# An attention and gated-MLP kernel: residual rows loaded during the attention products, input weights loaded in a chain, the last z2 normalised ahead of the weight scaling and stored from GpSimd's queue

## The chip, the cores and the metric

One core of a Trainium2 chip runs the whole kernel. The metric is the device time of one execution in microseconds (us); lower is better. A core has a matrix engine (PE, with its weight loads shown as PEld), a vector engine (DVE), a scalar engine (ACT), GpSimd (POOL), and a sync engine (SP) that mostly issues transfers. DMAs can be issued from SP, ACT and POOL; each of these queues works through its instructions in order, so an instruction that waits holds up all that stands behind it.

## The reference

Two blocks in a row on 2048 rows of 1024 columns, in bf16:

```
h   = x + attention(layernorm(x)) @ wo        # 32 heads of 32; each row sees 8 rows: itself, 2, 4 .. 14 back
z   = gelu(layernorm(h) @ w_in)               # 1024 -> 3584
z1  = z[:, :1792];  z2 = layernorm(z[:, 1792:])
g   = w_sp @ z2 + b_sp                        # w_sp is 2048 x 2048: it mixes the rows
out = h + (z1 * g) @ w_out                    # 1792 -> 1024
```

## The kernel before

The 2048 rows are worked in four chunks of 512 rows, and a chunk in four blocks of 128 rows. Up to line 1031 nearly all work is entered into a planner; after that comes the row-mixing product and the output projection, written out in order.

**The planner.** `Order` (line 69) takes operations with an engine, a cost in us, dependences with latencies, a priority (lower goes first) and slots (three PSUM accumulators `acc`, buffers and so on). `run` (line 85) plays the schedule with these costs and then calls the functions in order of planned start. So the order of instructions on every engine's queue follows from the planned times, not from when data really arrive. `dma_op` (line 396) is an operation of the pseudo-engine "DMA": its cost says how long a transfer is taken to last, and its function issues it at its planned start; with an empty function it is only a delay.

**Attention of a chunk** (`attention`, line 484). DVE forms q*k for eight shifts (L522 with the additions L526, L529, L532), PE sums over the head's columns (L552), softmax follows; the attention weights are spread to all partitions, the second half of them through HBM (`spread`, line 598). Then come eight products with v. The products with shifts 1 and 3 are added by DMAs issued from POOL (`gather`, line 651, into `av_y` and `av_oT`), the products 4 to 7 by DVE (`dm` L638, `plus` L646). The end is `G["avdone", c]`.

**Head of a chunk** (`head`, line 687). PE multiplies with `wo` (L709), four blocks, each in four parts. DVE adds the residual rows `xr` and sums (L718, `res`); the sum `hb` is stored to HBM (L720), ACT squares it (L723), and the normalised rows are transposed by DMA into `hnT` (L760; for the last chunk block by block, L741). `xr` has three buffers. Three blocks are loaded by `xr_load` (L713) when the first part of block 0's matmuls is emitted, the fourth after ACT has squared block 0.

**The weights of the first MLP product.** `load_win` (line 385) issues four loads from POOL's queue: k = 0 and 1 are the columns of z2, k = 2 and 3 those of z1; 2.0, 1.5, 2.0 and 1.5 MB. Loads 0 and 1 go into the buffers of q's and k's weights, so they can start when the last chunk's q and k products are done (lines 978, 979). Load 0 also waits for the spread of chunk 1 (`behind_spread`). Loads 2 and 3 are issued together by `open_` (line 971) when the last v product is done. Behind these loads on POOL's queue stands the load of v for chunk 2 (L493).

**z2 and z1** (`b_z2`, line 767; `b_z1`, line 842). For each block PE fills one accumulator with 1024 columns and one with 768 (L786); ACT applies gelu into `u` (L793) and squares it for the variance (L801); POOL takes the power -0.5 (L682). For chunks 0 to 2 the normalised z2 is written by ACT and stored from SP. For the last chunk (`each`) it is done block by block: DVE normalises (L820), and the store is issued from ACT's queue (L821). z1 follows with L852 and gelu L858.

**The row mixing's weights.** The rows of `w_sp` are transposed by DMA from SP into `rawa` and `rawb` (`load_raw`, L927), `rawa` in three pieces. DVE multiplies them with row factors (`scale_raw`, L932), forms four differences (`t_forms`, L939 to L945) and four forms of z2 (`z_form`, L962, from `z2f` loaded back at L954), and a bias row (L922); these are the inputs of a two-by-two block product with seven multiplications (L1051). In the last chunk the orders of these DVE operations come from the planner, with priorities 3.5 to 3.7 against 0.6 for L820.

Lines 1014 to 1017 give the raw loads' planned costs (2.2, 2.2, 5.5 and 9.0 us) and what they follow: a dependence `(G["hnT", 3, k], 0.0 - 3.9)` means "3.9 us before the planned end of block k's transpose", which lasts 4.0 in the plan, so just after its start.

Of the kernel before, what the change touches and what calls it, by code (L numbers as in the profile page):

```python
# [132 lines left out]
def kernel(  # L133
# [251 lines left out]
    def load_win(k, t):  # L385
        c0, wd = win_specs[k]
        i_ = dma_w(t[:], win_view[:, :, c0:c0 + wd])
        if k == 0:
            behind_spread(i_, 1)
        wins[k] = t  # L390

    o_ = Order({"PE": 22.4, "ACT": 23.6, "DVE": 15.4, "POOL": 12.0}, {"acc": 3, "L": 1, "prod": 1, "part": 2, "xn": 4})
# [88 lines left out]
    def behind_spread(i_, c):  # L481
        tc.add_manual_dep(i_.ins, G["spread_i", c].ins.name, wait_for, reason="keep a large load out of the spread weights' way")

    def attention(c):
# [174 lines left out]
        o_2 = dm(2, "oT", [z] + ([G["headmm", c - 1]] if c else []))  # L659
        z = dm(3, "zz", [o_2] + ([G["hnT", c - 1]] if c else []))  # L660
        g2 = gather("oT", "zz", [z], 15.0)
        prev = dm(4, "b", [z], take="prod")
        for w in (5, 6, 7):
            m_ = dm(w, "p", [prev], take="prod" if w == 5 else None, free="part" if w == 7 else None)
            prev = plus("b", "p", [m_], free="prod" if w == 7 else None)
# [21 lines left out]
    def head(c):  # L687
        last = c == NCH - 1
        st = {}
        hbs = []  # L690
        prio = 4.0 + c * 0.1
        xr0 = dma_op(0.0, lambda: None, [G["attq", c]] if ("attq", c) in G else [])
        sqd = []
        for il in range(TPC):
            i = c * TPC + il
            deps = [G["avdone", c]]
            for part in range(4):
                def mm(part=part, il=il, i=i):
                    if part == 0:
                        if il == 0:  # L700
                            st["hsum"] = bp.tile([P, TPC], FP32, name="hsum", tag="hsum")
                            st["hsq"] = bp.tile([P, TPC], FP32, name="hsq", tag="hsq")
                            st["hnc"] = bp.tile([P, TPC, D], BF16, name="hb", tag="hb", bufs=1)
                            for k in range(min(XRB, TPC)):
                                xr_load(k)
                        st["acc", il] = new_acc()
                    for dl in range(2 * part, 2 * part + 2):
                        for nh in range(2):
                            T.matmul(st["acc", il][:, nh, :], oTs[c][:, dl, il * P:(il + 1) * P], wo_sb[:, dl, nh * CH:(nh + 1) * CH],  # L709
                                     start=(dl == 0), stop=(dl == DLO - 1))  # L710
                def xr_load(k):
                    st["xr", k] = bp.tile([P, D], BF16, name="xr", tag="xr", bufs=XRB)
                    dma(st["xr", k][:], x2d[(c * TPC + k) * P:(c * TPC + k + 1) * P, :])  # L713
                m_ = add("PE", 0.8634, mm, deps, prio=prio + il * 1e-2 + part * 1e-3, take="acc" if part == 0 else None)
                deps = [(m_, 0.0)]
            def res(il=il, i=i):
                hb = st["hnc"][:, il, :]
                V.scalar_tensor_tensor(hb, st["acc", il][:].rearrange("p a b -> p (a b)"), 1.0, st["xr", il][:],  # L718
                                       op0=ALU.mult, op1=ALU.add, accum_out=st["hsum"][:, il:il + 1])
                dma(h_d[i * P:(i + 1) * P, :], hb)  # L720
            r_ = add("DVE", 1.15, res, [m_] + ([G["hdone", c - 1]] if c else []), prio=1.0, free="acc", lat=0.15)
            def hsq(il=il):
                A.activation(st["xr", il][:], st["hnc"][:, il, :], ACTF.Square, accum_out=st["hsq"][:, il:il + 1])  # L723
                if il + XRB < TPC:
                    xr_load(il + XRB)
            sqd.append(add("ACT", 1.12, hsq, [r_], prio=3.0, lat=0.25))
        G["headmm", c] = m_
        if last:
            G["close"] = dma_op(0.0, close_, [G["headmm", c]] + [G["z2n", k, il] for k in range(c) for il in range(TPC)])
            for il in range(TPC):  # L730
                rs = batch_rstd(("l2", c, il), lambda il=il: st["hsum"][:, il:il + 1], lambda il=il: st["hsq"][:, il:il + 1],
                                D, f"l2_{il}", [sqd[il]], 0.5, cols=1)
                def nrm(il=il):
                    t = G["l2", c, il]
                    V.tensor_scalar(st["hnc"][:, il, :], st["hnc"][:, il, :], t["nmean"][:], t["rstd"][:],
                                    op0=ALU.add, op1=ALU.mult)
                n_ = add("DVE", 0.5, nrm, [rs], prio=0.6)
                def tr(il=il):
                    if il == 0:
                        hnTs[c] = bp.tile([P, TPC, KT, P], BF16, name="hnT", tag="hn%d" % (c % 2), bufs=1)  # L740
                    nc.sync.dma_start_transpose(hnTs[c][:, il], st["hnc"][:, il, :].rearrange("s (a p) -> s a p", p=P))  # L741
                G["hnT", c, il] = dma_op(4.0, tr, [n_])
            G["hnT", c] = G["hnT", c, TPC - 1]
            G["hdone", c] = n_
            return
        rs = batch_rstd(("l2", c), lambda: st["hsum"][:], lambda: st["hsq"][:], D, "l2", sqd, 0.5)
        nd = []
        for il in range(TPC):
            def nrm(il=il):
                t = G["l2", c]  # L750
                if il < L2DVE[c]:
                    V.tensor_scalar(st["hnc"][:, il, :], st["hnc"][:, il, :], t["nmean"][:, il:il + 1], t["rstd"][:, il:il + 1],
                                    op0=ALU.add, op1=ALU.mult)
                else:
                    A.activation(st["hnc"][:, il, :], st["hnc"][:, il, :], ACTF.Identity, scale=t["rstd"][:, il:il + 1], bias=t["nb"][:, il:il + 1])
            nd.append(add("DVE", 0.5, nrm, [rs], prio=0.6) if il < L2DVE[c] else add("ACT", 1.16, nrm, [rs], prio=4.0))
        G["hdone", c] = nd[-1]
        def tr():
            hnTs[c] = bp.tile([P, TPC, KT, P], BF16, name="hnT", tag="hn%d" % (c % 2), bufs=1)
            nc.sync.dma_start_transpose(hnTs[c][:].rearrange("p il a s -> p (il a) s"),  # L760
                                        st["hnc"][:].rearrange("s il (a p) -> s (il a) p", p=P))
        G["hnT", c] = dma_op(8.0, tr, nd)
# [4 lines left out]
    def b_z2(c):  # L767
# [43 lines left out]
        for il in range(TPC):  # L811
# [5 lines left out]
            def nrm(il=il, i=i, part=1):  # L817
                if each:
                    t = G["l3", c, il]
                    V.tensor_scalar(st["u", il][:], st["u", il][:], t["nmean"][:], t["rstd"][:], op0=ALU.add, op1=ALU.mult)  # L820
                    A.dma_start(z2_d[i * P:(i + 1) * P, :], st["u", il][:])  # L821
                    return
                t = G["l3", c]
                z2 = st["u", il]
                if Z2ACT[c] > il:
                    cols = slice(part * FH // 2, (part + 1) * FH // 2)
                    A.activation(z2[:, cols], st["u", il][:, cols], ACTF.Identity, scale=t["rstd"][:, il:il + 1], bias=t["nb"][:, il:il + 1])
                else:
                    V.tensor_scalar(z2[:], st["u", il][:], t["nmean"][:, il:il + 1], t["rstd"][:, il:il + 1], op0=ALU.add, op1=ALU.mult)
                if part:  # L830
                    dma(z2_d[i * P:(i + 1) * P, :], z2[:])
# [153 lines left out]
    for c in range(NCH):  # L985
        attention(c)
        if c == 1:
            G["win", 0].deps.append((G["spread", 1], 0.1))
        if c < NCH - 1:
            head(c)  # L990
    for c in range(NCH - 1):
# [19 lines left out]
    rl_ = dma_op(4.0, rows_first, [(ro_, 2.5), G["close"]])  # L1011
    b_z2(NCH - 1)
    b_z1(NCH - 1)
    r0_ = dma_op(2.2, lambda: load_raw(0, 0, 1), [G["close"], rl_.deps[0], (G["hnT", NCH - 1, 1], 0.0 - 3.9)])
    r0_ = dma_op(2.2, lambda: load_raw(0, 1, 2), [r0_, (G["hnT", NCH - 1, 2], 0.0 - 3.9)])
    r0_ = dma_op(5.5, lambda: load_raw(0, 2, TPC), [r0_, (G["hnT", NCH - 1, 3], 0.0 - 3.9)])
    r1_ = dma_op(9.0, lambda: load_raw(1), [r0_])
    prev = []
    for c, r_ in ((0, r0_), (1, r1_)):
        for k0 in (0, HK):  # L1020
            prev = [add("DVE", 2.3, lambda c=c, k0=k0: scale_raw(c, k0), [r_, rl_] + prev, prio=3.5)]
    for n in (0, 3, 1, 2):
        prev = [add("DVE", 2.3, lambda n=n: t_forms(0, n), prev, prio=3.6)]
    z_ld = {}
    for n in range(2):
        for hf in range(2):
            z_ld[n, hf] = dma_op(6.0, lambda n=n, hf=hf: load_z2f(n, hf), [r1_] + [G["z2st", 2 * hf + c, il] for c in range(2) for il in range(TPC)])
    for m in (3, 1, 2, 4):
        prev = [add("DVE", 0.7, lambda m=m: z_form(0, m), [z_ld[0, 0]] + ([z_ld[0, 1]] if m != 3 else []) + prev, prio=3.65)]
    add("DVE", 0.7, lambda: bias_rows(0), prev, prio=3.7)  # L1030
    o_.run()
    wout_a = wtile([P, 8, D], "wout_a", "wA")
# [188 lines left out]
```

## Time and profile before

| | us |
|---|---|
| runs shown: 714.1, 712.27, 713.95; median | 713.95 |
| the profiled execution | 714.85 |
| its span, first to last instruction | 712.9 |
| PE busy | 696.4 |
| DVE busy | 507.1 |
| ACT busy | 276.0 |
| POOL busy | 119.4 |
| mean granted clock of PE | 0.993 |

A line of the timeline gives start, duration, engine, line, operation, out<-in, shapes and a count of instructions merged; in brackets how long the engine stood idle before it and what released it. "SPq", "ACTq" and "POOLq" are the instructions of the queues themselves, such as the issue of a DMA. The stages of the profiled span, by what PE works on:

| us from the span's start | PE's work |
|---|---|
| 0 to 191 | q, k, v of all four chunks; chunk 0's `wo` product at 116 to 130 |
| 191 to 202 | z2 of chunk 0, first block |
| 202 to 216 | `wo` product of chunk 1 |
| 216 to 387 | z2 and z1 of chunks 0 to 2, `wo` products of chunks 2 (286 to 300) and 3 (372 to 386) |
| 387 to 418 | z2 of chunk 3, the last |
| 418 to 443 | z1 of chunk 3 |
| 443 to 710 | row mixing and output projection, twice |

Idle time of an engine that is not the one that others wait for costs nothing; here PE is busy for 98% of the span.

### The profile page before, as it was taken

The page shows a single profiled execution, that of the slowest core. Times are in us where ns is not written, and L with a number is a line of the kernel's source. Part 1 is how long each engine was busy: PE and PEld are TensorE (multiplying, and loading weights), DVE is VectorE, ACT ScalarE, POOL GpSimd, SP SyncE. Part 2 cuts the span into 40 slices and gives each one's busy share as a digit, 9 for nine tenths or more (in the row PEclk, how much of TensorE's full clock was granted, in tenths as well). Part 3 has the DMA queues.
Part 4 walks back from the last instruction along what each step waited for, and adds up shares of the span by engine and source line. Part 5 has one row for each costly group of instructions (what it writes and reads, how often), then busy time and mean ns, then how long its engine had stood idle before and what let it go on. Part 6 is the DMA issues. An engine that isn't in the chain of part 4 may idle for free.

```text
span 712.9 us, 8790 instructions
## 1 busy us (share of the span) xinstructions
PE 696.4 (98%) x3400; PEld 360.5 (51%) x3427; DVE 507.1 (71%) x614; ACT 276.0 (39%) x388; POOL 119.4 (17%) x109
## 2 busy tenths in 40 slices
PE   8999999999989999999999989999999999999998
PEld 7766665666535445444444434444444444444444
DVE  6899899999959899997985275555454965554322
ACT  4546652443317786755663262135410001111000
POOL 0100010012101111100301020343340023434000
PEclk9999999999999999999999989999999999999999
DMA  9978597577991569361675975568999416352121
GB/s 324 322 237 231 171 224 237 148 206 193 309 395 49 147 203 274 137 191 38 134 244 143 213 228 160 177 188 227 308 296 212 157 59 175 92 152 85 44 89 45
DMA packets 145545, 133.04 MB, mean 187 GB/s; under 512 B 68768, under 2 KB 117312, under 8 KB 145376
## 3 DMA queue, kind: packets, MB, share of 16 engines
q1 hardware_dynamic: 132784, 88.93, 44.5%
q0 software_dynamic: 7488, 31.13, 15.7%
q10 hardware_dynamic: 5232, 12.42, 5.1%
q8 instruction: 27, 0.44, 0.3%
q14 instruction: 14, 0.11, 0.0%
HBM read 75.24 MB, written 33.10 MB: 152 GB/s over the span
## 4 chain that ended last, share of the span: by engine, by line
PE 88%; DVE 6%; DMA 4%; issue 1%; ACT 1%; SPq 1%; ACTq 0%; DVEq 0%
PE bank L1051 24%; PE acc L459 21%; PE bank L1152 14%; PE acc L852 12%; PE acc L786 8%; PE acc L709 6%; DMA xr<-in_A_x_dram 2%; PE acc L303 2%; DVE prod L522 2%; DMA rawa<-in_B_w_sp_dram 1%; DVE prod L526 1%; DVE hb L718 1%; DVE prod L529 1%; DVE part L532 0%; DMA xp<-in_A_x_dram 0%
## 5 line engine op out<-in xcount | busy, mean ns | idle before, releaser
L786 PE MATMUL acc<-win,hnT 128*128 128x512 bf16 (+1 forms) x501 | 101.5, 361 | 9.3 <-ACT u L793 4.7
L852 PE MATMUL acc<-hnT,win 128*128 128x512 bf16 x448 | 98.0, 379 | 0.0
L786 PEld LDWEIGHTS <-hnT 128*128 128x128 bf16 x512 | 51.0, 100 | 58.9 <-issue 8.4
L522 DVE TENSOR_TENSOR prod<-qT,kT 128x4096 bf16<-128x4096 bf16 x32 | 72.7, 2283 | 1.3 <-ACT kT L465 1.3
L1152 PEld LDWEIGHTS <-zg 128*128 128x128 bf16 x462 | 44.6, 98 | 52.2
L1051 PEld LDWEIGHTS <-zs 128*128 128x128 f16 x448 | 43.8, 98 | 52.9
L852 PEld LDWEIGHTS <-win 128*128 128x128 bf16 x448 | 43.6, 98 | 52.5 <-issue 0.6
L470 ACT CAST stg<-acc 128x1024 bf16<-128x1024 f32 x36 | 36.4, 1012 | 61.2 <-PE acc L459 55.9
L1087 ACT COPY p<-bank 128x512 f32<-128x512 f32 x14 | 8.2, 586 | 132.0 <-PE bank L1051 129.6
L1152 PE MATMUL bank<-wout_a,zg 128*128 128x512 bf16 (+2 forms) x258 | 57.9, 373 | 0.3
L459 PE MATMUL acc<-xnT,wk 128*128 128x512 bf16 x256 | 56.5, 380 | 0.0
L709 PE MATMUL acc<-wo_sb,av_oT 128*128 128x512 bf16 x250 | 56.2, 381 | 0.3
L459 PE MATMUL acc<-xnT,wv 128*128 128x512 bf16 x256 | 56.1, 379 | 0.0
L1155 DVE SCALAR_TENSOR_TENSOR hr<-bank,rinv_w,hr 128x512 bf16<-128x512 f32 (+2 forms) x33 | 22.8, 730 | 44.8 <-PE bank L1152 43.6
L1051 PE MATMUL bank<-rawa,z2f 128*128 128x512 f16 x224 | 52.9, 379 | 1.1 <-ACT z1s L858 1.1
L1051 PEld LDWEIGHTS <-z2f 128*128 128x128 bf16 x336 | 32.8, 98 | 40.9 <-issue 1.4
L1051 PE MATMUL bank<-rawb,zs 128*128 128x512 f16 x224 | 52.9, 379 | 0.0
L1051 PE MATMUL bank<-form,zs 128*128 128x512 f16 x224 | 50.6, 379 | 0.0
L459 PEld LDWEIGHTS <-wv 128*128 128x128 bf16 x256 | 36.6, 143 | 18.6 <-issue 0.2
L459 PEld LDWEIGHTS <-wk 128*128 128x128 bf16 x256 | 36.5, 144 | 18.8 <-issue 0.7
L1152 PE MATMUL bank<-wout_b,zg 128*128 128x512 bf16 (+2 forms) x194 | 44.2, 373 | 0.2
L858 ACT ACTIVATE z1s<-acc 128x1024 bf16<-128x1024 f32 x28 | 28.6, 1022 | 38.0 <-PE acc L852 29.4
(188 smaller groups left out, 942.5 us busy)
## 6 DMA issues: line engine op xcount, KB each, us to landing
z2f<-z_d SPq DMA_DIRECT2D x28, 512.0 KB, 5.4
qkv_d<-stg SPq DMA_DIRECT2D x36, 256.0 KB, 3.8
wn<-in_B_w_sp_dram ACTq DMA_DIRECT2D x16, 512.0 KB, 3.7
z1c<-z_d SPq DMA_DIRECT2D x14, 512.0 KB, 4.1
z_d<-z1s SPq DMA_DIRECT2D x21, 256.0 KB, 2.2
z_d<-u SPq DMA_DIRECT2D x12, 448.0 KB, 2.5
av_y<-av_z POOLq DMA_DIRECT2D x4, 1024.0 KB, 9.8
av_oT<-av_zz POOLq DMA_DIRECT2D x4, 1024.0 KB, 15.1
```

The lines of the kernel that those rows point to most:

```text
L303: T.matmul(dst.rearrange("p (a b) -> p a b", b=P), wqs[:, kt, dl, :], xnT[0][:, lo:hi, kt, :], start=start, stop=stop)
L459: T.matmul(G[key][:, j, :].rearrange("p (a b) -> p a b", a=TPC), wv[:, kt, dl, :], xnT[c][:, :, kt, :], start=(kt == 0), stop=(kt == KT - 1))
L470: A.copy(stg[:], G[key][:])
L522: V.tensor_tensor(st["prod"][:], qT[:], kT[:, :, o:o + CH], op=ALU.mult)
L709: T.matmul(st["acc", il][:, nh, :], oTs[c][:, dl, il * P:(il + 1) * P], wo_sb[:, dl, nh * CH:(nh + 1) * CH], start=(dl == 0), stop=(dl == ...
L786: T.matmul(accf[:, n0:n1], hnTs[c][:, il, kt, :], wins[hf][:, kt, n0:n1], start=(kt == 0), stop=(kt == KT - 1))
L852: T.matmul(G["accy", c, fp][:, j, :].rearrange("p (a b) -> p a b", a=TPC), wt[:, kt, f0 * P:(f0 + 1) * P], hnTs[c][:, :, kt, :], start=(kt ...
L858: A.activation(z1s[:], G["accy", c, fp][:], ACTF.Gelu_apprx_tanh)
L1051: T.matmul(dst[:], wts[:, k, :], mov[:, k, :], start=(first and k == 0), stop=(k == HK - 1), skip_group_check=not first)
L1087: A.copy(p1[:], k1[:])
L1152: T.matmul(outs, zg[:, f, il * P:(il + 1) * P], wt[:, f0, lo:hi], start=(f == 0), stop=(f == NF - 1))
L1155: V.scalar_tensor_tensor(hr[:, lo:hi], acc[:, 0:hi - lo], rv[:, t:t + 1], hr[:, lo:hi], op0=ALU.mult, op1=ALU.add)
```

## The change

Four edits:

1. The first three residual blocks `xr` of each chunk are loaded by an operation of their own, planned right after DVE's product with shift 4 (`G["avmid", c]`), instead of with the first matmuls of `wo`.
2. The loads of the input weights 1 and 2 each wait for the one before (a dependence on its landing, in the program and in the plan). Load 3 follows load 2 without such a wait.
3. The store of z2 in the last chunk is issued from POOL's queue (`dma_w`) instead of ACT's.
4. The planned costs of the raw loads become 4.0, 4.0, 8.0 and 10.5 us; the first follows the transpose of block 2 instead of block 1, the second that of block 3 instead of block 2. The loads of z2 (`z_ld`) are entered earlier, and one z2 form is placed between the differences.

```
 def load_win(k, t):                                   # edit 2
         behind_spread(i_, 1)
+    elif k < 3:
+        tc.add_manual_dep(i_.ins, G["win_i", k - 1].ins.name, wait_for, reason="one load of input weights after the other")
+    G["win_i", k] = i_
...
+        G["win", 1].deps.append((G["win", 0], 0.1))
+        G["open"].deps.append((G["win", 1], 0.1))
...
-    prev = dm(4, "b", [z], take="prod")               # edit 1
+    prev = G["avmid", c] = dm(4, "b", [z], take="prod")
...
-    xr0 = dma_op(0.0, lambda: None, [G["attq", c]] if ("attq", c) in G else [])
+    def xr_load(k):
+        st["xr", k] = bp.tile([P, D], BF16, name="xr", tag="xr", bufs=XRB)
+        dma(st["xr", k][:], x2d[(c * TPC + k) * P:(c * TPC + k + 1) * P, :])
+    def xr_first():
+        for k in range(XRB):
+            xr_load(k)
+    xr0 = dma_op(4.0, xr_first, [G["avmid", c]] + ([G["hdone", c - 1]] if c else []))
...
-                A.dma_start(z2_d[i * P:(i + 1) * P, :], st["u", il][:])      # edit 3
+                dma_w(z2_d[i * P:(i + 1) * P, :], st["u", il][:])
...
-r0_ = dma_op(2.2, lambda: load_raw(0, 0, 1), [G["close"], rl_.deps[0], (G["hnT", NCH - 1, 1], 0.0 - 3.9)])   # edit 4
-r0_ = dma_op(2.2, lambda: load_raw(0, 1, 2), [r0_, (G["hnT", NCH - 1, 2], 0.0 - 3.9)])
-r0_ = dma_op(5.5, lambda: load_raw(0, 2, TPC), [r0_, (G["hnT", NCH - 1, 3], 0.0 - 3.9)])
-r1_ = dma_op(9.0, lambda: load_raw(1), [r0_])
+r0_ = dma_op(4.0, lambda: load_raw(0, 0, 1), [G["close"], rl_.deps[0], (G["hnT", NCH - 1, 2], 0.0 - 3.9)])
+r0_ = dma_op(4.0, lambda: load_raw(0, 1, 2), [r0_, (G["hnT", NCH - 1, 3], 0.0 - 3.9)])
+r0_ = dma_op(8.0, lambda: load_raw(0, 2, TPC), [r0_, (G["hnT", NCH - 1, 3], 0.0 - 3.9)])
+r1_ = dma_op(10.5, lambda: load_raw(1), [r0_])
...
-for n in (0, 3, 1, 2):
+for n in (0, 3):
     prev = [add("DVE", 2.3, lambda n=n: t_forms(0, n), prev, prio=3.6)]
+prev = [add("DVE", 0.7, lambda: z_form(0, 3), [z_ld[0, 0]] + prev, prio=3.6)]
+for n in (1, 2):
+    prev = [add("DVE", 2.3, lambda n=n: t_forms(0, n), prev, prio=3.6)]
-for m in (3, 1, 2, 4):
+for m in (1, 2, 4):
     prev = [add("DVE", 0.7, lambda m=m: z_form(0, m), [z_ld[0, 0], z_ld[0, 1]] + prev, prio=3.65)]
```

In head, L718 (`res`) now also depends on `xr0` in the plan.

More of the change, by code (lines that the diff above doesn't have):

```diff
@@ L703, in mm @@
                             st["hnc"] = bp.tile([P, TPC, D], BF16, name="hb", tag="hb", bufs=1)
-                            for k in range(min(XRB, TPC)):
-                                xr_load(k)
                         st["acc", il] = new_acc()
@@ L710, in mm @@
                                      start=(dl == 0), stop=(dl == DLO - 1))
-                def xr_load(k):
-                    st["xr", k] = bp.tile([P, D], BF16, name="xr", tag="xr", bufs=XRB)
-                    dma(st["xr", k][:], x2d[(c * TPC + k) * P:(c * TPC + k + 1) * P, :])
                 m_ = add("PE", 0.8634, mm, deps, prio=prio + il * 1e-2 + part * 1e-3, take="acc" if part == 0 else None)
@@ L720, in res @@
                 dma(h_d[i * P:(i + 1) * P, :], hb)
-            r_ = add("DVE", 1.15, res, [m_] + ([G["hdone", c - 1]] if c else []), prio=1.0, free="acc", lat=0.15)
+            r_ = add("DVE", 1.15, res, [m_, xr0] + ([G["hdone", c - 1]] if c else []), prio=1.0, free="acc", lat=0.15)
             def hsq(il=il):
@@ L1021 @@
             prev = [add("DVE", 2.3, lambda c=c, k0=k0: scale_raw(c, k0), [r_, rl_] + prev, prio=3.5)]
-    for n in (0, 3, 1, 2):
-        prev = [add("DVE", 2.3, lambda n=n: t_forms(0, n), prev, prio=3.6)]
     z_ld = {}
@@ L1027 @@
             z_ld[n, hf] = dma_op(6.0, lambda n=n, hf=hf: load_z2f(n, hf), [r1_] + [G["z2st", 2 * hf + c, il] for c in range(2) for il in range(TPC)])
-    for m in (3, 1, 2, 4):
-        prev = [add("DVE", 0.7, lambda m=m: z_form(0, m), [z_ld[0, 0]] + ([z_ld[0, 1]] if m != 3 else []) + prev, prio=3.65)]
+    for n in (0, 3):
+        prev = [add("DVE", 2.3, lambda n=n: t_forms(0, n), prev, prio=3.6)]
+    prev = [add("DVE", 0.7, lambda: z_form(0, 3), [z_ld[0, 0]] + prev, prio=3.6)]
+    for n in (1, 2):
+        prev = [add("DVE", 2.3, lambda n=n: t_forms(0, n), prev, prio=3.6)]
+    for m in (1, 2, 4):
+        prev = [add("DVE", 0.7, lambda m=m: z_form(0, m), [z_ld[0, 0], z_ld[0, 1]] + prev, prio=3.65)]
     add("DVE", 0.7, lambda: bias_rows(0), prev, prio=3.7)
```

## The prediction

> **What bounds the kernel now.** I read the page first. TensorE (PE) is busy for 696.4 of 712.9 us, so a change can only win back PE's idle time and time at a lowered clock. The list of PE's waits (us in total, times, longest) names the idle time that there is; it stands below the page's line:
>
> ```profile
> PE 696.4 (98%) x3400; PEld 360.5 (51%) x3427; DVE 507.1 (71%) x614; ACT 276.0 (39%) x388; POOL 119.4 (17%) x109
> ```
>
> ```profile
> PE acc L786 <- ACT u L793: 4.7, 1, 4.7
> PE acc L786 <- DMA win<-in_B_w_in_dram: 4.0, 1, 4.0
> ...
> PE bank L1051 <- ACT z1s L858: 1.1, 1, 1.1
> ...
> PE L L552 <- DVE part L532: 0.3, 1, 0.3
> ```
>
> Two waits count. I call the 4.0 us the first stall (after 194 us) and the 4.7 us the last-chunk stall (after 408 us). The table by stages shows the clock beside each (columns: PE, PEld, DVE, ACT, POOL busy, granted clock, DMA share, GB/s):
>
> ```profile
> 200.00:202.00 2.00, 2.00 (x8) 0.98 (x7) 0.82 (x1) 0.00 (x0) 0.00 (x0) 0.50 1.02 408
> ...
> 410.00:420.00 10.00, 6.87 (x26) 3.27 (x26) 6.92 (x14) 8.15 (x13) 0.88 (x2) 0.66 1.15 309
> ```
>
> After each stall the matmuls run at a granted clock of 0.5 to 0.7 for a few us, so a stall costs more than its wait. The rest of the last-chunk stall is in the timeline:
>
> ```profile
> 406.92 2.29 DVE L932 TENSOR_TENSOR rawa<-rawa,rows 128x4096 f16<-128x4096 bf16 x1 [10.91 <-DMA rawa<-in_B_w_sp_dram]
> 409.13 0.74 DVE L820 TENSOR_SCALAR u<-u,l_0nmean,l_0rstd 128x1792 bf16<-128x1792 bf16 x1
> ...
> 409.91 0.34 ACTq L821 DMA_DIRECT2D z_d<-u  x1
> 410.29 1.70 ACT L801 ACTIVATE junk<-u 128x1792 bf16<-128x1792 bf16 x1 [10.43 <-DVE u L820]
> ...
> 413.13 5.02 PE L786 MATMUL acc<-win,hnT 128*128 128x512 bf16 x16 [4.70 <-ACT u L793]
> ```
>
> Read it upwards. PE wants a free accumulator, which ACT's gelu (L793) frees. ACT stands at its own DMA instruction, the store of z2 (L821), which waits for DVE's normalisation L820. L820 has had its factor since 396.63 (POOL's L682 at 396.09 took 0.54), but it is queued behind L932, which waits for `rawa` until 406.92.
>
> **The last chunk's z2, step by step.** Both edits hit this. The store goes to GpSimd's queue, so ACT no longer stands behind it. And with the planner's new times for the raw loads (4, 4, 8, 10.5 us for 2.2, 2.2, 5.5, 9.0, each gated one transpose later or after the one before), the plan's `rawa` is due 0.1 + 4.0 + 8.0 and more, over 12 us after the last transpose's start instead of 0.1 + 5.5, while block 0's factor came 6.1 us after that transpose had its input (390.55 in the trace); so I expect L820 of block 0 to stand ahead of L932. The stall goes even if only the store moves. PE would run from 386.81: block 0 took 6.07 us (32 matmuls to 392.88), four take 24.3, end 411.1. In the trace z2 ends at 418.15. Its loss is 4.70 of waiting and 5.02 - 2.62 = 2.40 us at the low clock: **-7.1 us**. ACT keeps up: per block it needs 1.02 + 0.81 + 1.70 and three reads of 0.19, 4.1 us, below 6.07.
>
> What is late next? First the transposes `hnT` of blocks 2 and 3, on SP. The first raw load (4.03 us of SP) moves behind block 2's transpose, so that is issued near 389.2 instead of 393.49, and block 3's near 394.6 instead of 397.00. At 6.7 us to landing (the upper row of `hnT`) they are there at 396 and 401; PE wants them at 399 and 405. All raw loads together still end on SP near 412, so `rawb` lands near 416.4 as now. Then DVE's chain: from 416.4 the four remaining big operations (two scalings, of which one waits for block 3's norm, and so on) are 2 x 2.29 (L932), 0.74 (L820), 4 x 2.29 (L939 to L945), 4 x 0.69 (L962) and 0.68 (L922): 17.9 us, ending 434.3. PE reaches L1051 at 443.44 - 7.1 = 436.3, and wants the last forms 3 to 5 us later still. Now the same chain ends at 440.1 against 443.44, so the cover shrinks from 3.3 us to 2.0 and does not break.
>
> The store on GpSimd's queue: this trace has no such store. An issue there takes 0.88 to 1.27 us (L387, L493, L652) where ACT's took 0.34. Behind it on that queue stands only the next block's small L682. Landing: 2.5 us (the same rows on SP) or 4.3 (on ACT) on one end, 21.0 (`win` on GpSimd's queue, in a full stage) on the other; I take 4.3, the same store in the same stage, because the DMA share is 0.26 at 420 to 430. The last one is issued at about 420.4 and lands at 424.7; `z2f` follows in 5.4 (430.1); its first reader (L962, second form) is needed by PE at 439.7, so 0.7 + 5.4 back the store may land as late as 433.6: 13.2 us of landing are hidden. Cost 0.
>
> The row against this edit is L682: 0.54 us on an idle DVE, 2.52 at 419.66 and 426.14, beside a 2.28 us DVE operation. The Trainium skill, page "SBUF — State Buffer", section "SBUF: two separate sides", goes further: it warns that a DMA issued from GpSimd can't get its descriptors written while DVE runs in certain modes, and advises the ACT or SP queue. By that rule each of the four issues could be held to the end of a DVE operation, 2.3 us by the row; the last would land at 427 and still be hidden. The `win` issue at 172.16 took 0.95 us beside DVE's L635, which doesn't show it.
>
> **The chained weight loads.** I split the DMA view into 2 us windows and added up each queue's bytes. GpSimd's queue q0 works its transfers off one by one: the landings (issue plus time to landing) are `win` 0 at 188.0, the gather into `av_oT` 194.0, `win` 1 198.8, `win` 2 205.0, `win` 3 210.7, `vT` 214.2, in the order of issue, and the bytes between fit one transfer each. So `win` 1 (issued 177.79, landing 21.0 us later) is not slowed by `win` 2 and 3; it stands behind the gather. Chained, it is issued near 189, when `win` 0 has landed, while the gather works until 194.0: no hole, the same landing. `win` 2 waits for 198.8, leaves about 2 us of hole, and lands near 207, `vT` near 216; L852 wants `win` 2 at 235.16 and attention wants `vT` after 250. GpSimd queues nothing else behind these waits until 221.14. **0 us** for the chain. A bound below: if transfers shared the queue, the whole first stall would go (4.03 of waiting, 12 matmuls in 3.33 us instead of 1.97, 64 of L709 in 14.23 instead of 13.81): 5.8 us.
>
> **The residual rows.** They are now issued after the product with the fifth shift, about 177 instead of 192.83 in chunk 1, between the stores of q and k to HBM on SP, at a time when all DMA engines are full:
>
> ```profile
> q0 software_dynamic: 176, 0.66, 80.2%
> q1 hardware_dynamic: 175, 0.16, 23.4%
> ...
> q0 software_dynamic: 118, 0.54, 71.1%
> q1 hardware_dynamic: 120, 0.22, 30.4%
> ```
>
> The first pair is 196:198, the second 206:208. The queues alternate packet for packet; SP's take 23.4% of 16 x 2 us / 175 = 0.043 us when they are stores of 1 KB, 0.081 when `xr` (2 KB) comes. Three `xr` are 384 packets: 384 x 0.038 / 16 = 0.9 us more ahead of the gather and of `win` 1. So DVE loses its 7.33 us wait for `xr`, but PE's first stall grows: **+0.9 us** (bounds: 0, if packets pass in slots that q0 leaves, and 1.9, all 0.79 MB at 413 GB/s). DVE being 1 to 2 us earlier after 208 saves L552's **-0.3 us**, nothing else: PE runs on from 202.12 to 243.88 without a wait. The stores behind `xr` land about 6 us later; ACT's cast of four stores on reuses the buffer, so one cast slips from 191.38 to about 196, hidden since PE then waits for `win` 1 until 199. In chunk 0 the same push meets casts that have 5.7 us before PE misses an accumulator: hidden, though barely. Chunks 2 and 3 load `xr` early already or with the DMA half idle: 0.
>
> **Sum**: -7.1 + 0.9 - 0.3 = -6.5 us on the profiled 714.85 (span 712.9), 708.35. The median shown, 713.95, is 0.9 below the profiled run; 713.95 - 6.5 gives **707.5 us**. A measurement of this kernel can tell about 0.3% (2.1 us) from no change.
>
> **Rivals.** (a) The chain pays: if `win` 1 shared bandwidth with later loads, the first stall goes: 713.95 - 7.1 - 5.8 - 0.3 = 700.8. Against it: landings in order of issue. 0.08. (b) The gain is halved: the stores pushed behind `xr` hold ACT's casts in chunk 0 or 1 until PE lacks an accumulator (2 to 4 us), or a transpose is late for blocks 2 and 3: about 710.5. For it: landings of those stores are at 11 to 14 us already. 0.14. (c) Slower: the last z2 store lands late on GpSimd's queue. From 13.2 us to landing it decides; at 21.0 us (`win`'s row) `z2f` comes at 446.8, the forms at 447.5 against 439.7, PE stands 7.8 us and pays some 1.5 at a low clock: 713.95 - 6.5 + 9.3 = 716.8. Against: an idle DMA there. 0.06. (d) The change doesn't do what it says: ACT still meets a wait of 10 us in the last chunk, for example since block 0's norm stays behind L932 and something on ACT still needs it: 713.95 + 0.9 - 0.3 = 714.6. 0.06. The forecast, 704.5 to 709.5, has 0.66.
>
> Faster by over 0.3% (below 711.8): 0.66 + 0.08 + 0.10 of (b) = 0.84; within 0.3%: 0.10; slower: 0.06. The range for 8 in 10 takes in the forecast, most of (b) and some of (a): 702.0 to 711.5.
>
> **What would show it.** Right: no wait of ACT for L820 near 400, L820 of block 0 before the first L932, z2's last chunk in 24.3 us, L1051 starting near 437 with the same wait of about 1 us; `win` 1 landing at 198 to 200, PE's wait for it 4 to 5 us; no wait of L718 for `xr` over 1 us. Wrong: a first stall under 2 us (a), waits of L459 for ACT (b), L1051 or L962 waiting for `z2f` (c).

## The result and the profile after

| | before | after |
|---|---|---|
| median of 7 runs each, us | 714.1 (712.27 to 715.58) | 708.65 (707.63 to 711.23) |
| ratio, 95% interval | | 0.9926 [0.9907, 0.9945] |
| the profiled execution | 714.85 | 711.23 |
| its span | 712.9 | 709.2 |
| mean granted clock | 0.993 | 0.995 |

The change gains 5.45 us, or 0.7%; the forecast was a gain of 6.5 (707.5 us). The profiled execution is the slowest of the seven after; the other six lie between 707.63 and 708.91. Line numbers from 390 on have grown by 3 to 9: L786 is now L790, L793 L797, L801 L805, L820 L824, L821 L825, L932 L936, L962 L966, L1051 L1060; L709 is L716 and L718 is L722.

The page's line of busy time, kernel after:

```profile
PE 695.8 (98%) x3427; PEld 359.8 (51%) x3427; DVE 508.8 (72%) x614; ACT 276.6 (39%) x388; POOL 120.5 (17%) x113
```

PE's waits after (us in total, times, longest):

```profile
PE acc L790 <- DMA win<-in_B_w_in_dram: 6.7, 1, 6.7
PE bank L1060 <- DVE zs L966: 1.3, 1, 1.3
```

The 4.7 us for ACT are gone, and the wait for `win` has grown from 4.0 to 6.7. One stall is removed, and another is longer. The 1.3 us for `zs` stand at 574.98, in the second pass of the row mixing, after DVE had waited 11.64 us for a bias row; a second profile of the same kernel (e9 below) does not have this wait, so I don't count it to the change.

The last chunk's z2 in the timeline after:

```profile
388.94 24.38 PE L790 MATMUL acc<-win,hnT 128*128 128x512 bf16 x128
...
398.96 0.75 DVE L824 TENSOR_SCALAR u<-u,l_0nmean,l_0rstd 128x1792 bf16<-128x1792 bf16 x1 [0.66 <-POOL l_0rstd L685]
400.28 0.66 POOL L825 DMA_DIRECT2D z_d<-u  x1 [1.36 <-ACT u L797]
...
402.18 1.70 ACT L805 ACTIVATE junk<-u 128x1792 bf16<-128x1792 bf16 x1
...
411.34 2.29 DVE L936 TENSOR_TENSOR rawa<-rawa,rows 128x4096 f16<-128x4096 bf16 x1 [5.56 <-DMA rawa<-in_B_w_sp_dram]
```

All 128 matmuls run as one stretch of 24.4 us. DVE normalises block 0 (L824) as soon as its factor is there, ahead of L936 (the 0.66 us are DVE's wait for that factor); DVE still waits for `rawa`, but nothing that PE needs stands behind that. GpSimd issues the store at 400.28, and ACT squares the next block at 402.18 (L805, no wait in brackets) where it stood for 10.43 us before.

The first stall, GpSimd's timeline after:

```profile
172.32 1.04 POOL L387 DMA_DIRECT2D win<-in_B_w_in_dram  x1
...
190.95 0.93 POOL L387 DMA_DIRECT2D win<-in_B_w_in_dram  x1 [14.52 <-DMA win<-in_B_w_in_dram]
```

The chain is seen in the bracket: load 1 is issued at 190.95, when load 0 has landed, where before it was issued at 177.79. It lands at 201.7, before at 198.8; the prediction had said 198 to 200. The matmuls that wait for it start at 201.72 instead of 198.79:

```profile
201.72 3.76 PE L790 MATMUL acc<-win,hnT 128*128 128x512 bf16 x12 [6.70 <-DMA win<-in_B_w_in_dram]
```

How the DMA queues looked from 192 to 194 (queue: packets, MB, share of 16 engines):

```profile
q1 hardware_dynamic: 261, 0.47, 62.6%
q0 software_dynamic: 51, 0.15, 37.2%
```

and the same 2 us before:

```profile
q0 software_dynamic: 143, 0.58, 77.1%
q1 hardware_dynamic: 146, 0.14, 20.7%
```

q0, GpSimd's queue, moved 0.15 MB after and 0.14 in the next 2 us; before, it moved 0.58 and 0.69. That is a hole of the kind that the prediction denied. Whether it is what makes load 1 late is a question for the experiments.

### The profile page after: what moved, and what is told of

Same layout as the page of the kernel before. It is cut to its first block, busy times and chain, and to the rows that moved or that the text cites. A ratio compares the mean times of both kernels' runs of the same rounds, so it can differ in the third digit from the quotient of the medians.

```text
span 709.2 us, 8835 instructions
## 1 busy us (share of the span) xinstructions
PE 695.8 (98%) x3427; PEld 359.8 (51%) x3427; DVE 508.8 (72%) x614; ACT 276.6 (39%) x388; POOL 120.5 (17%) x113
## 4 chain that ended last, share of the span: by engine, by line
PE 66%; DMA 2%; DVE 2%; issue 1%; SPq 0%; ACT 0%; DVEq 0%
PE bank L1060 24%; PE acc L856 14%; PE acc L790 13%; PE bank L1161 9%; PE acc L716 6%; DMA win<-in_B_w_in_dram 2%; DVE hr L1164 1%; DVE rawa L936 1%; DMA out_dram<-hr 0%; DMA brow<-in_B_b_sp_dram 0%; SPq L931 0%; DVE rawb L936 0%; DVE form L945 0%; DVE form L943 0%; PE L L555 0%
## 5 line engine op out<-in xcount | busy, mean ns | idle before, releaser
L790 PE MATMUL acc<-win,hnT 128*128 128x512 bf16 (+1 forms) x512 | 99.8, 357 | 6.7 <-DMA win<-in_B_w_in_dram 6.7
L790 PEld LDWEIGHTS <-hnT 128*128 128x128 bf16 x512 | 50.4, 99 | 55.5 <-DMA win<-in_B_w_in_dram 7.2
L1060 PEld LDWEIGHTS <-zs 128*128 128x128 f16 x448 | 43.8, 98 | 54.4 <-DVE zs L966 1.8
L716 PE MATMUL acc<-wo_sb,av_oT 128*128 128x512 bf16 x256 | 56.1, 379 | 0.0
L1060 PE MATMUL bank<-rawb,zs 128*128 128x512 f16 x224 | 52.9, 379 | 1.3 <-DVE zs L966 1.3
L1060 PE MATMUL bank<-rawa,z2f 128*128 128x512 f16 x224 | 52.9, 379 | 1.1 <-ACT z1s L862 1.1
L1060 PEld LDWEIGHTS <-z2f 128*128 128x128 bf16 x336 | 32.9, 98 | 40.9 <-issue 1.4
L1060 PE MATMUL bank<-form,zs 128*128 128x512 f16 x224 | 50.6, 379 | 0.0
L462 PEld LDWEIGHTS <-wv 128*128 128x128 bf16 x256 | 36.6, 143 | 18.7 <-issue 0.2
```

The source lines that it names most:

```text
L462: T.matmul(G[key][:, j, :].rearrange("p (a b) -> p a b", a=TPC), wv[:, kt, dl, :], xnT[c][:, :, kt, :], start=(kt == 0), stop=(kt == KT - 1))
L790: T.matmul(accf[:, n0:n1], hnTs[c][:, il, kt, :], wins[hf][:, kt, n0:n1], start=(kt == 0), stop=(kt == KT - 1))
L1060: T.matmul(dst[:], wts[:, k, :], mov[:, k, :], start=(first and k == 0), stop=(k == HK - 1), skip_group_check=not first)
```

## The experiments

Each kernel below is the kernel before with only the edit named, unless it says otherwise. Times are medians; each ratio compares with runs of the kernel before on the same chip. Line numbers move by a few from kernel to kernel.

**Which edit removes the last-chunk stall?** The theory: either moving the store (edit 3) or moving DVE's order (edit 4) is enough, since the stall needs both an ACT that stands at the store and a DVE that is late with L820. The rival: the stall comes from ACT's work itself or from a late transpose.

e1, edits 3 and 4 together:

```
-                A.dma_start(z2_d[...], st["u", il][:])
+                dma_w(z2_d[...], st["u", il][:])
...
-r0_ = dma_op(2.2, lambda: load_raw(0, 0, 1), [..., (G["hnT", NCH - 1, 1], 0.0 - 3.9)])
+r0_ = dma_op(4.0, lambda: load_raw(0, 0, 1), [..., (G["hnT", NCH - 1, 2], 0.0 - 3.9)])
```

(and the rest of edit 4 as in the diff above)

> Edits 3 and 4 alone (z2's store from GpSimd's queue, planned times of the raw loads), the residual rows and the weight loads as before. My theory: these two carry the whole gain. z2 of the last chunk takes 24.3 us without a wait, 7.1 us less than before; PE's first stall stays at 4.0 us. Time 714.1 - 7.1 = 707.0, at or a little below the changed kernel's 708.65. Rival (the chain and the early residual rows also give something): slower than the changed kernel, 710 or more.

Measured 708.02 against 713.34, ratio 0.992 [0.9907, 0.9934]. No wait of PE for ACT, z2 in 24.38 us. These two edits carry the whole gain, as the theory says. One thing is not as expected: PE's first stall is 5.4 us in this profile and not 4.0, though the loads are as before.

e4, edit 3 alone (the first two lines of that diff).

> Edit 3 alone: only the store of the last chunk's z2 moves from ACT's to GpSimd's queue, the planner's order of the raw loads and of DVE is unchanged. My theory: the stall goes even so, since ACT no longer stands behind DVE: PE's wait of 4.7 us in the last chunk is gone, z2 takes 24.3 us or up to 1 us more (the transposes of blocks 2 and 3 stay late on SP), time 707 to 708. Rival (the order is what matters): the stall stays, 714.

Measured 708.03 against 713.34, ratio 0.9926 [0.9913, 0.994]. Its timeline:

```profile
399.94 1.70 ACT L801 ACTIVATE junk<-u 128x1792 bf16<-128x1792 bf16 x1
...
402.46 1.02 ACT L793 ACTIVATE u<-acc 128x1024 bf16<-128x1024 f32 x1 [0.73 <-PE acc L786]
...
407.04 2.29 DVE L932 TENSOR_TENSOR rawa<-rawa,rows 128x4096 f16<-128x4096 bf16 x1 [10.98 <-DMA rawa<-in_B_w_sp_dram]
409.25 0.74 DVE L820 TENSOR_SCALAR u<-u,l_0nmean,l_0rstd 128x1792 bf16<-128x1792 bf16 x1
```

DVE is as late as before: L820 of block 0 at 409.25, behind 10.98 us of waiting for `rawa`. But ACT squares at 399.94 and applies gelu at 402.46, and PE's z2 runs in 24.38 us, since the store that waits for L820 is GpSimd's now. The last store goes out at 430.04, 7 us later than after, and DVE's second z2 form then ends at 438.8 for matmuls that begin at 439.81, so this version has about 1 us in hand.

e5, edit 4 alone; the store stays on ACT's queue.

> Edit 4 alone: DVE's order changes (blocks 0 and 1 are normalised ahead of the weight scaling), the store of z2 stays on ACT's queue. My theory: edits 3 and 4 each remove the last-chunk stall by themselves, since with this order ACT's store of block 0 waits 2 us instead of 10; for blocks 2 and 3 ACT stands up to 6 us, which the three accumulators cover but for 0 to 2 us of PE. Time 707 to 709. Rival: only moving the store off ACT counts, the stall comes back at blocks 2 and 3: 711 or more.

Measured 708.41 against 714.48, ratio 0.9914 [0.9888, 0.994]. ACT still stands at the store of block 2, for 3.99 us at 416, and at that of block 3 for 3.27 us, but PE has accumulators left and doesn't wait. So the two edits remove the same stall, and either is enough; they don't add up.

**What do the loads cost?** The theory: the chain 0, the early rows about +0.6 net. The rivals: the chain pays, or the pushed stores hold ACT's casts.

e2, edit 2 alone:

```
+        elif k < 3:
+            tc.add_manual_dep(i_.ins, G["win_i", k - 1].ins.name, wait_for, reason=...)
...
+            G["win", 1].deps.append((G["win", 0], 0.1))
+            G["open"].deps.append((G["win", 1], 0.1))
```

> Edit 2 alone, the chained weight loads. My theory on record: GpSimd's queue works its transfers off one by one, weight load 1 is issued near 189 while the gather still works and lands at 198.8 as before; PE's first wait stays at 4.0 us, time 714.1 (0 us). Rival from the trace of the changed kernel: the DMA engines that finish the gather early find nothing behind it, since load 1's descriptors come late; load 1 lands 1 to 2 us later, first wait 5 to 6 us, time 715 to 716.5. The intent's theory (loads share bandwidth): the first stall of 5.8 us goes, 708.

Measured 713.33 against 713.34, ratio 1.0 [0.9985, 1.0015]. Load 1, issued at 188.51, landed at 198.7; PE waited 3.8 us for it. So the rival of a later load 1 and that of shared bandwidth are both out. The last chunk is not edited here, and its stall is there, but smaller. Timeline of e2:

```profile
405.91 2.29 DVE L935 TENSOR_TENSOR rawa<-rawa,rows 128x4096 f16<-128x4096 bf16 x1 [9.34 <-DMA rawa<-in_B_w_sp_dram]
...
412.11 4.44 PE L789 MATMUL acc<-win,hnT 128*128 128x512 bf16 x16 [3.12 <-ACT u L796]
```

z2's start is at 387.21 in it, so `rawa` released DVE 18.7 us after it, where in the profile of before it was 406.92 - 386.65 = 20.3.

e3, edit 1 alone:

```
+    prev = G["avmid", c] = dm(4, "b", [z], take="prod")
...
+    xr0 = dma_op(4.0, xr_first, [G["avmid", c]] + ([G["hdone", c - 1]] if c else []))
```

> Edit 1 alone, the residual rows loaded in the attention products. My theory on record: 384 packets of 2 KB instead of 1 KB ahead of the gather and of weight load 1 put 0.9 us on PE's first wait (4.0 to 4.9), L552's 0.3 us goes: 714.7. Rival: the early rows carry all of the 2.7 us by which the first wait grew in the changed kernel: wait 6.7 us, time 716.5. DVE's wait for the residual rows (7.3 us) is gone in both.

Measured 714.43 against 713.34, ratio 1.0017 [1.0007, 1.0027]: +1.2 us [0.5, 1.9]. PE waited 5.1 us for `win` and, in the unedited last chunk, 3.6 us for ACT.

To see the pair of load edits without the last-chunk stall, three kernels ran on one chip, beside 713.98 for the kernel before. e9 is the whole change again.

> The whole change once more, beside the two kernels that leave out one early edit each. In its first profile PE's first wait was 6.7 us, against 5.1 with the early rows alone and 3.8 with the chain alone. Theory: the two add up to more than their sum, since the early rows delay weight load 0, the chain holds load 1's issue until load 0 has landed, and the DMA engines that have finished the gather then have nothing behind it. Wait 6 to 7 us, time 1 to 1.6 us above the kernel without the chain. Rival: chance of one execution; wait about 5, time equal to the kernel without the chain.

Measured 708.93 (707.9 to 709.43), ratio 0.9924 [0.9907, 0.9942]; PE's first wait is 6.1 us.

e10 is the change without edit 2.

> Edits 1, 3 and 4, weight loads as before. Both theories: PE's first wait about 5.1 us as with the early rows alone, time some 0.9 to 1.2 us above edits 3 and 4 alone by the ratio (0.992 + 0.0015 = 0.9935).

Measured 707.83 (707.21 to 708.91), ratio 0.9913 [0.9893, 0.9932]; the first wait is 5.6 us.

e11 is the change without edit 1.

> Edits 2, 3 and 4, residual rows as before. Theory: the chain alone costs nothing, PE's first wait is about 4 us, ratio 0.992, the fastest of the three on this chip. Rival (the chain costs by itself): ratio 0.994 or more.

Measured 708.13 (706.65 to 708.55), ratio 0.9913 [0.9895, 0.9931]; the first wait is 5.3 us, not 4. Taking either edit out gains 1.1 or 0.8 us in the medians, but the intervals overlap. The traces say more. The table has, for the one profile of each kernel (e6 to e8 and e12 are described below), how long load 0 took from its issue (at about 172 in all), when the gather behind it and when load 1 landed, and what lies between these two, each to about 0.1 us:

| loads | kernel | load 0 took | gather landed | load 1 landed | between |
|---|---|---|---|---|---|
| as before | before | 15.8 | 194.0 | 198.8 | 4.8 |
| | e4 | 16.1 | 194.5 | 199.2 | 4.7 |
| | e5 | 17.8 | 195.1 | 199.9 | 4.8 |
| | e1 | 17.5 | 195.3 | 200.1 | 4.8 |
| | e8 | 16.2 | 195.1 | 199.8 | 4.8 |
| chain | e2 | 15.8 | 194.0 | 198.7 | 4.7 |
| | e11 | 17.8 | 195.5 | 200.2 | 4.7 |
| rows after shift 4 | e3 | 15.9 | 194.3 | 199.9 | 5.6 |
| | e6 | 15.8 | 194.2 | 199.8 | 5.6 |
| | e10 | 15.5 | 194.9 | 200.3 | 5.4 |
| rows after shift 4, and chain | e9 | 17.8 | 195.2 | 200.5 | 5.3 |
| | after | 18.1 | 196.5 | 201.7 | 5.2 |
| rows after shift 0 | e7 | 18.1 | 196.7 | 201.5 | 4.7 |
| | e12 | 17.5 | 195.1 | 199.8 | 4.7 |

I had taken the longer first stall for the work of chain and rows together. The numbers of that theory came true in e9 (6.1 us of wait, 1.1 us in the medians), but the table doesn't bear it out: with both edits, 5.2 and 5.3 us lie between gather and load 1, no more than with the rows alone. Load 0 takes either 15.5 to 16.2 or 17.5 to 18.1 us, and both occur with the loads as before. Where it is late, load 1 lands later too: by 0.7 us with the loads as before (200.0 against 199.3 in the mean) and by 1.5 with the chain. The rows after shift 4 put load 1 back by 0.7 us with an early load 0 (200.0 against 199.3) and by 1.0 with a late one (201.1 against 200.1), 0.4 to 0.9 of it between the gather and load 1. Rows after shift 0 add nothing there. The chain changes neither: between gather and load 1 lie 4.7 us with it and 4.7 to 4.8 without it. The profile of before has an early load 0, both profiles of the whole change a late one; only this kernel was profiled twice, so whether load 0 changes from one execution to the next isn't shown.

**Is the first stall needed at all?** PE stops after 16 matmuls on load 0 because the planner thinks that load 1 lasts 10 us, while it takes 21 from issue. Theory: told 21 us, the planner lets PE use load 0's columns for a second accumulator and begin `wo` before load 1's columns; the rival: it only trades this wait for one on the gather or on `xr`.

e6 has edits 1, 3 and 4, and

```
-    G["win", 1] = dma_op(10.0, lambda: load_win(1, ...), [G["wdone", 3, 1]])
+    G["win", 1] = dma_op(21.0, lambda: load_win(1, ...), [G["wdone", 3, 1]])
```

> Edits 1, 3 and 4 without the chain, and one planned cost changed: weight load 1 is taken to last 21 us instead of 10 (as it does). The planner then puts block 1's first z2 columns (which need only weight load 0) ahead of block 0's second, so PE has work while load 1 is under way: 24 matmuls of load 0, then the wo product, then load 1's columns. My theory: the first stall of 5.8 us shrinks to the wait for the gather (the wo product starts at 198 to 199 in place of 196.3): 1 to 2 us. Time 708.3 - 4 = 704. Rival (the stall turns into a wait for the residual rows or an accumulator): 707 or more.

Measured 704.11 against 714.48, ratio 0.9864 [0.9835, 0.9893], as the theory said. Its profiled execution, 708.75, is 4.6 above that median, so I read no waits from it.

e7 is e6 with `xr` loaded earlier still, after the product with shift 0:

```
-    y = dm(0, "y", [], take="part")
+    y = G["avmid", c] = dm(0, "y", [], take="part")
```

> As the kernel before in this list, but the residual rows are planned after the product with shift 0 instead of shift 4, some 9 us earlier, when the DMA share is 0.3 to 0.6. My theory: they then land ahead of the full stage and add nothing to the gather and the weight loads: the wo product starts near 197, PE's wait below 1 us. Time 703 to 703.5. Rival (the place of the rows does not matter): equal to the kernel with the rows after shift 4.

Measured 703.4, ratio 0.9844 [0.9815, 0.9873]. The time is the forecast one, but PE waits 1.9 us for `av_oT` where the theory had less than 1, and none for `win`. The interval overlaps that of e6, so that shift 0 is a better place than shift 4 is not shown by the times.

e8 is e6 without edit 1: `xr` with the first matmuls, as before.

> Edits 3 and 4 and the 21 us for weight load 1, with the residual rows left where they were (issued with the wo product's first matmuls). My theory: now DVE's wait for the rows reaches PE: the wo product starts at 196.3 to 197, its third block wants an accumulator at 203, but DVE frees the first only when the rows land at 208; PE stands 5 to 6 us there, so the gain of the planned cost is lost: 707 to 708. Rival (the rows are hidden anyway, as in the kernel before): 703.

Measured 709.95, ratio 0.9935 [0.9912, 0.9959], 2 us more than forecast; why it is that much isn't known. The theory is right that DVE's wait for the rows now reaches PE, and the rival is out, as the timeline of e8 shows:

```profile
208.33 1.23 DVE L718 SCALAR_TENSOR_TENSOR hb<-acc,xr 128x1024 bf16<-128x1024 f32 x1 [6.47 <-DMA xr<-in_A_x_dram]
...
209.62 6.75 PE L709 MATMUL acc<-wo_sb,av_oT 128*128 128x512 bf16 x23 [5.02 <-DVE hb L718]
```

PE starts `wo` at 197.52, 4.6 us earlier than before, and in the middle of it stands 5.02 us for DVE, which has no residual rows. The wait for `xr` that was free in the kernel before is now on the path: there the early load (edit 1) is worth 709.95 - 704.11 = 5.8 us.

e12 has edit 3, `xr` after shift 0 and the 21 us, without the chain and without edit 4.

> The kernel with the rows after shift 0 and 21 us planned for weight load 1, but with edit 3 alone instead of 3 and 4 (raw loads and DVE's order as before). Theory: the order is worth nothing once the store is off ACT; DVE's last z2 form is done within 1 us of when PE wants it, so the ratio stays at 0.985 to 0.986. Rival: without the order DVE's forms come late for the row mixing, PE waits 1 to 3 us at its start, ratio 0.987 to 0.989.

Measured **702.51** (702.1 to 704.51) against 713.98, ratio 0.9843 [0.9822, 0.9863], granted clock 1.000. The ratio is that of e7 (0.9844), which has edit 4 too, so the order is worth nothing that these runs can tell once the store is off ACT; DVE's second z2 form ends at 430.4 here for matmuls that begin at 434.53, a wider margin than the 1 us of the theory. Its timeline:

```profile
191.12 5.34 PE L787 MATMUL acc<-win,hnT 128*128 128x512 bf16 x24
197.56 13.99 PE L713 MATMUL acc<-wo_sb,av_oT 128*128 128x512 bf16 x64 [1.10 <-DVE av_oT L646]
```

and the stage from 186 to 216 in the table by stages (PE, PEld, DVE, ACT, POOL busy, clock, DMA share, GB/s), first after, then e12:

```profile
186.00:216.00 30.00, 23.30 (x104) 11.64 (x103) 20.25 (x17) 6.73 (x9) 3.56 (x4) 0.89 0.93 309
```

```profile
186.00:216.00 30.00, 28.90 (x139) 14.37 (x138) 27.04 (x29) 9.90 (x16) 3.25 (x4) 1.00 0.99 346
```

PE works 5.6 us more in these 30 and at the full granted clock. The DMA share, 0.93 after, is 0.99.

## Why the prediction was right or wrong

**Last-chunk stall: right in mechanism, too large in size.** ACT no longer stands at the store, L824 of block 0 is ahead of L936, z2 runs in 24.4 us, and "the stall goes even if only the store moves" is e4. But -7.1 us came from one profile. PE's lines in it, with z2 (L786) and the start of z1 (L852):

```profile
386.65 21.78 PE L786 MATMUL acc<-win,hnT 128*128 128x512 bf16 x110
413.13 5.02 PE L786 MATMUL acc<-win,hnT 128*128 128x512 bf16 x16 [4.70 <-ACT u L793]
417.99 24.34 PE L852 MATMUL acc<-hnT,win 128*128 128x512 bf16 x112
```

and the same in e3, whose last chunk is unedited:

```profile
387.56 21.78 PE L787 MATMUL acc<-win,hnT 128*128 128x512 bf16 x112
412.91 4.12 PE L787 MATMUL acc<-win,hnT 128*128 128x512 bf16 x16 [3.57 <-ACT u L794]
416.87 24.34 PE L853 MATMUL acc<-hnT,win 128*128 128x512 bf16 x112
```

From z2's start to z1's start the profile of before took 31.34 us; e3 took 29.31 and e2, also unedited there, 29.18, against 24.2 without the stall. So the stall costs 5.1 and 5.0 us in those, and 7.1 in the one I read. DVE stands until the last of the three pieces of `rawa` has landed (20.3 us after z2's start, against 18.7 in e2 and 19.2 in e3), and the matmuls behind the wait lost 2.40 us to the low clock, against 1.82 in e2 and 1.50 in e3. The times agree with the smaller size: e1, e4 and e5 gain 5.3, 5.3 and 6.1 us in their medians.

**Chain: 0, right; "no hole" was wrong.** In all four profiles with the chain q0 moves less from 192 to 194 (0.07 to 0.34 MB against 0.58). I let load 1 flow from the moment the gather ends, but q0 is back at 0.67 to 0.70 MB in 2 us only some 3 to 6 us after load 1's issue. What I had not seen is that this costs nothing (to within 1.1 us, by e2's interval): load 1 lands 4.7 to 4.8 us behind the gather in e2 and e11, as in the kernel before. Whether the chain costs something once the rows are early, as the 1.1 us between e9 and e10 may say, stays open: the intervals overlap, and "between" is 5.2 to 5.6 us with the rows whether chained or not. The hole has a use that I overlooked: SP's queue q1 moved 331 packets in it in e2 (192 to 194) against 146 before, and the residual rows, issued at 193 in both, landed in 7.7 to 8.0 us instead of 15.2 to 18.5. DVE's wait for them, 7.33 us before, is gone with the chain alone; in e2 and e11 DVE waits for PE's `wo` product instead.

**Residual rows: right in sign, about right in size.** +1.2 us [0.5, 1.9] alone, +0.7 to +1.0 in the landing of load 1, against +0.9 forecast. PE's wait for `win`, 6.1 and 6.7 us where I forecast 4 to 5, has about 1 us of this, and about 1 us goes with the late load 0, which the prediction did not have; the rest of the 6.7 us stays open. The -0.3 for L552 can't be put down to the rows: that wait is gone from PE's list after, but also from those of e2 and e4, whose rows are as before.

**Sum.** -6.5 was forecast and -5.45 measured. With -5.3 from e4 and +1.2 from e3 it would be -4.1, with -6.1 from e5 it would be -4.9; the interval of the measured -5.45, from -6.6 to -3.9 by its ratio, takes in both sums and the forecast. The step that failed is the size of the first term: 7.1 us put down, 5.0 to 5.1 in two other profiles and 5.3 to 6.1 in the times. That the forecast is only 1 us off, with a first term that is 1.0 to 2.1 us too large, is partly chance: the whole change gained more than its terms do when they are measured apart.

**Covers: right.** The DVE chain ends at 437.4 (434.3 forecast, 436.6 with the 2.3 us by which the chunk starts later), and in this pass PE waits for none of it; L1060 starts at 438.61 with the same wait of 1.1. The last z2 store was issued at 423.05, not 420.4. The four stores on GpSimd's queue landed after 4.6 to 6.5 us, where I took 4.3 and 13.2 was the point from which (c) decides: rival (c) is out. Issues took 0.58 to 0.66 us, less than the 0.88 I took as the lower end. The wait of L552 is gone from PE's list, as forecast. Rival (a) falls with e2, (d) with L824 of block 0 at 398.96 and e1, and of (b) there is no sign: PE waits for no cast and no transpose.

The rule that I weighed against edit 3 (the Trainium skill, page "SBUF — State Buffer", section "SBUF: two separate sides") speaks of certain modes of DVE, and no run here shows whether L936 works in one; the issues of the last two stores were not held beside it:

```profile
419.09 2.38 POOL L685 TENSOR_TENSOR l_3rstd<-l_3var,nhalf 128x1 f32<-128x1 f32 x1
...
422.17 2.28 DVE L936 TENSOR_TENSOR rawb<-rawb,rows 128x4096 f16<-128x4096 bf16 x1
423.05 0.59 POOL L825 DMA_DIRECT2D z_d<-u  x1 [1.58 <-issue]
```

In this timeline of after GpSimd's small power at 419.09 takes 2.38 us beside another L936 (from 418.77), against 0.54 on an idle DVE, but the store's issue at 423.05 takes 0.59 beside the same operation, and its data landed in 4.6 us.

## What to carry to other kernels

A DMA issue that waits for another engine belongs on a queue behind which nothing urgent stands; on a busy engine's queue it turns that engine's order into the other's (here 0.34 us of issue cost 5 to 7 us of PE). A planner's cost for a load must be the time that it takes in the stage where it runs: one number, 21 us for 10, was worth another 3.5 us with the early residual rows (e6 against e10, by their ratios on two chips) and nothing without them (e8), and the rows paid only with it. Whether the chain, which also brings the rows in early, would do as well as edit 1 with the 21 us was not tried. And size a stall from several profiles: the one that is read may have its worst case.

## What was not expected of the hardware

The same load at the same place took 15.5 to 16.2 or 17.5 to 18.1 us, in fourteen profiles nothing between, and both occurred with the loads as before; what decides it was not tried. And the size of a stall in unedited code varied by 2.1 us between three profiles (each of another kernel, with edits elsewhere), not only by its wait: after 4.7 us of it the clock stood at 0.50, 0.50 and 0.56 in the three 2 us steps from 412 in the profile of before, after 3.6 us at 0.57, 0.57 and 1.00 in e3.
